# Attention and gated MLP on one core: row tiles 4 and 5 are loaded transposed, and the opening's loads and statistics stand in another order

## The chip, the core and the metric

The kernel runs on one core of a Trainium2 chip. A core has TensorE (PE in the profile; it multiplies matrices and, with an identity as operand, transposes), VectorE (DVE), ScalarE (ACT), GpSimd (POOL) and SyncE (SP), which here only issues transfers. Each engine works through its own list of instructions in order and waits on semaphores for the others. Transfers run on 16 DMA engines. The metric is the device time of one execution in microseconds (us); the time of a kernel is the median of its runs.

## The reference

x has 2048 rows (positions) of 512 numbers. Cut to what matters here:

```python
xn = _layernorm(x, axis=-1)              # every row: minus its mean, times its rstd
s = _A_ref(xn, A_wqkv, A_wo)             # qkv = xn @ wqkv; 32 heads, 8 positions back in steps of 2
g = _silu(_B_ref(xn, B_w_in, B_w_sp, B_b_sp, B_w_out))
return x + s * g
# _B_ref: z = gelu(xn @ w_in); z1 | z2 = its halves; z2 = layernorm(z2)
#         out = (z1 * (w_sp @ z2 + b_sp)) @ w_out
```

Everything begins with the normalised rows xn, and PE needs them with the 512 features on the partitions, that is, transposed.

## The kernel before

**Tiles.** Tile j of the 16 row tiles holds rows p * 16 + j, with p = 0 to 127 on the partitions. Matrices are multiplied in float32 accuracy by three products: every operand is split into a high part (an ACT copy to the type fp32r) and a low part (a DVE subtraction), and high x high, high x low and low x high are added. A tile against one group of 512 columns of wqkv takes 4 blocks of features x 3 = 12 matmuls of 512 columns. There are three such groups; the part of the program in question is the first 60 us, groups 0 and 1. Behind it come group 2, the two halves of the MLP and the spatial product (w_sp), with the attention's DVE and GpSimd work beside them, and the output projection.

**Two ways to a transposed tile.** Tiles 0 to 5 (`OPEN = 6`) come in by rows (`load_x`). DVE takes mean and variance (`stats_x`, L214 and L215), GpSimd the power -1/2 (`rstd_x`, L221), DVE subtracts the mean (and for tiles 4 and up multiplies by rstd) (`normal_x`, L228, L197), PE transposes four 128 x 128 blocks into a PSUM bank (`turned_x`, L234), ACT copies the high part (L235), DVE makes the low part (`low_x`, L240). For tiles 0 to 3 rstd is applied later.

Tiles 6 to 15 come in twice. By rows (`fetch_rows`, L257) only for their statistics (`row_stats`, L261 and L262). By columns from an input that holds x transposed (`fetch_cols`, L268), which needs the mean and rstd of each row along the free dimension, on every partition. They get there over DRAM: power on GpSimd (`rows_ready`, L272 and L273), a small DVE transpose of the table `mvx` of all tiles' statistics (`rows_out`, L244), four small stores of it to `mv_d` (L246), and one load that broadcasts it to all partitions (`rows_in`, L277). Then DVE subtracts and multiplies in two operations of 128 x 512 (`column_tile`, L286), ACT copies the high part (L289) and DVE makes the low part.

**What sets the order.** Instructions given through `pin` stay, on each engine, in the order in which the code is written: all the above, and the loads on SP. The products behind the opening (`product`, L395 to L397) and the evictions with their stores (`pair`, L443 and L452) are not pinned; the scheduler puts them where its own timeline has their operands ready. SP issues in order, so a load that waits for a free buffer holds up what stands behind it. Row tiles by `fetch_rows` have 6 buffers, column tiles 4, the broadcast rows 2, the small transpose's result 1.

**The opening** (`opening`, L301) writes PE's order out by hand: `times(j, ...)` (L314) gives single matmuls of tile j in group 0, and tile j + 1's transposes stand between tile j's high and low parts. `raw1` are the four loads of group 1's weights, which `weights(1, ...)` splits when the opening ends. The finished products of tiles 0 to 4 are kept in `first`; `pair(0, j)` evicts them two at a time.

## Time and profile before

| what | us |
|---|---|
| median of 3 runs | 692.48 |
| lowest, highest run | 691.8, 693.27 |
| the profiled execution, its own time | 692.16 |
| its span, first to last instruction | 690.3 |
| granted TensorE clock, mean | 1.000 |
| PE, DVE, ACT, POOL busy | 684.8, 619.8, 276.0, 216.8 |

The profile is of one execution, 692.16 us long, of which 690.3 lie between its first and last instruction. PE's busy time is a model of overlapping matmuls, so a busy PE says only that there was no hole in its work; how fast it advances is read from the distance between the starts of its instructions. In rows in order of time the columns are start, duration, engine, line, operation, tile written <- tiles read, shapes, count, and in brackets the idle time before and what ended it. SPq and ACTq are transfers issued by these engines; an issue's row says nothing of when the data lands. In rows of stretches the columns are the stretch, its length, the busy time of PE, PE's weight loads (PEld), DVE, ACT and POOL with counts, the granted clock, the share of the DMA engines and GB/s. A name in these rows leaves out tile numbers, so `qkv<-wqkv_0h` may be of any group, and 0 there is the block of features.

### The profile page before, as it was taken

The numbers are of one execution on the slowest core, as the hardware profiler recorded it, in microseconds if no ns is written. First come the engines' busy times: TensorE is split into PE (matmuls) and PEld (weight loads), VectorE is DVE, ScalarE is ACT, GpSimd is POOL, SyncE is SP. The second block draws the span as 40 slices with busy tenths as digits, with TensorE's granted clock in tenths as the row PEclk, the third lists the DMA queues.
The fourth block names the chain that finished last, engine by engine and source line by source line (L and its number), as shares of the span: only waits on it lengthen the run. The fifth ranks groups of instructions, "written<-read, shape, count | busy, mean of one in ns | idle before, by whom it ended". The sixth has DMA issues, their size and how long they took to land.

```text
span 690.3 us, 9237 instructions
## 1 busy us (share of the span) xinstructions
PE 684.8 (99%) x3080; PEld 572.5 (83%) x3080; DVE 619.8 (90%) x866; ACT 276.0 (40%) x458; POOL 216.8 (31%) x242
## 2 busy tenths in 40 slices
PE   9999999999999999999999999999999999999997
PEld 7888888888888899888888888888888888888886
DVE  6677869999989979798999999999999999999765
ACT  4343334224424256785434544432444444211432
POOL 3105837373443221223323222224021202552320
PEclk9999999999999999999999999999999999999999
DMA  8759899969999865267797859677576692663996
GB/s 281 257 180 299 292 359 388 334 218 370 404 414 355 324 207 180 97 207 249 232 397 285 328 195 319 202 237 262 171 270 238 219 325 89 205 186 126 308 309 252
DMA packets 102223, 182.43 MB, mean 264 GB/s; under 512 B 9184, under 2 KB 45152, under 8 KB 102176
## 3 DMA queue, kind: packets, MB, share of 16 engines
q1 hardware_dynamic: 56624, 102.21, 43.7%
q0 software_dynamic: 13824, 52.24, 20.9%
q10 hardware_dynamic: 31728, 27.40, 11.9%
q8 instruction: 24, 0.39, 0.2%
q14 instruction: 23, 0.19, 0.1%
HBM read 122.49 MB, written 59.32 MB: 263 GB/s over the span
## 4 chain that ended last, share of the span: by engine, by line
PE 99%; DMA 0%; DVE 0%; issue 0%
PE g L848 39%; PE qkv L395 6%; PE qkv L396 6%; PE qkv L397 6%; PE z L751 4%; PE z L750 4%; PE z L715 4%; PE z L714 4%; PE b L1089 4%; PE b L1091 4%; PE b L1090 4%; PE z L716 4%; PE z L749 3%; PE s L1089 2%; PE s L1091 2%; PE s L1090 2%
## 5 line engine op out<-in xcount | busy, mean ns | idle before, releaser
L643 POOL TENSOR_TENSOR pv<-pv 128x1024 f32<-128x1024 f32 x29 | 69.6, 2399 | 94.3 <-DVE pv L630 83.0
L583 DVE TENSOR_TENSOR pr<-k,q 128x2048 f32<-128x2048 f32 x32 | 74.7, 2333 | 1.5 <-DMA k<-qkv_d 1.4
L630 DVE TENSOR_TENSOR pv<-v,lg 128x2048 f32<-128x2048 f32 x32 | 74.5, 2329 | 0.6
L590 DVE TENSOR_REDUCE lg<-pr 128x128 f32<-128x2048 f32 x32 | 72.9, 2279 | 0.1
L657 POOL DMA_DIRECT2D o_d<-tt x32 | 17.9, 560 | 148.0 <-DVE tt L656 104.5
L443 ACT ACTIVATE stage<-qkv 128x512 f32<-128x512 f32 x40 | 23.0, 590 | 31.9 <-DMA qkv_d<-stage 20.2
L1100 ACT ACTIVATE bt<-b 128x512 f32<-128x512 f32 x16 | 9.5, 596 | 45.7 <-PE b L1091 45.7
L830 POOL DMA_DIRECT2D ol<-o_d x32 | 17.7, 554 | 28.9 <-DVE o_1l L204 6.0
L720 ACT ACTIVATE z1t<-z 128x512 f32<-128x512 f32 x28 | 15.5, 596 | 25.8 <-DMA z_d<-z1t 14.1
L761 DVE BATCH_NORM_STATS2 zst<-zt 128x6 f32<-128x448 f32 x32 | 19.3, 610 | 7.0 <-ACT zt L752 7.0
L751 PE MATMUL z<-w_0h,BIG 128*128 128x512 f32 x64 | 25.0, 391 | 0.0
L750 PE MATMUL z<-w_0l,BIG 128*128 128x512 f32 x64 | 25.0, 391 | 0.0
L286 DVE TENSOR_TENSOR xT<-xT,mr 128x512 f32<-128x512 f32 x20 | 14.9, 743 | 11.2 <-DMA mr<-mv_d 6.9
L775 ACT ACTIVATE zt<-zt,nmz,mvz 128x896 f32<-128x896 f32 x16 | 17.4, 1128 | 18.0 <-POOL nmz L769 18.0
L767 POOL TENSOR_TENSOR mvz<-mvz,nhalf 128x2 f32<-128x2 f32 x8 | 9.3, 1157 | 47.3 <-DVE mvz L764 47.3
L749 PE MATMUL z<-w_0h,BIG 128*128 128x512 f32 x60 | 23.3, 389 | 0.0
L648 DVE TENSOR_TENSOR pv<-pv 128x512 f32<-128x512 f32 x32 | 22.9, 714 | 0.0
L752 ACT ACTIVATE zt<-z 128x512 f32<-128x512 f32 (+1 forms) x32 | 16.0, 537 | 15.8 <-DMA sums_d<-sa 12.2
L751 PE MATMUL z<-w_1h,BIG 128*128 128x384 f32 x64 | 21.5, 336 | 0.0
L750 PE MATMUL z<-w_1l,BIG 128*128 128x384 f32 x64 | 21.5, 335 | 0.0
L403 POOL TENSOR_TENSOR sb<-sa,sb 128x512 f32<-128x512 f32 x12 | 19.8, 1647 | 5.4 <-DMA sb<-in_w_sp 5.0
L202 ACT ACTIVATE BIG<-zl 128x512 fp32r<-128x512 f32 x20 | 12.4, 630 | 20.7 <-DVE zl L921 20.6
(480 smaller groups left out, 2262.6 us busy)
## 6 DMA issues: line engine op xcount, KB each, us to landing
qkv_d<-stage ACTq DMA_DIRECT2D x24, 512.0 KB
v<-qkv_d POOLq DMA_DIRECT2D x14, 704.0 KB, 5.0
k<-qkv_d POOLq DMA_DIRECT2D x13, 704.0 KB, 6.3
sums_d<-sa POOLq DMA_DIRECT2D x14, 512.0 KB, 7.6
sums_d<-sb POOLq DMA_DIRECT2D x14, 512.0 KB, 9.4
z_d<-z1t ACTq DMA_DIRECT2D x14, 512.0 KB
zl<-z_d SPq DMA_DIRECT2D x12, 512.0 KB
tr<-t_d SPq DMA_DIRECT2D x12, 384.0 KB
```

The lines of the kernel that those rows point to most:

```text
L395: nc.tensor.matmul(pq, xh[:, k], wh, start=k == 0, stop=False)
L396: nc.tensor.matmul(pq, xh[:, k], wl, start=False, stop=False)
L397: nc.tensor.matmul(pq, xl[:, k], wh, start=False, stop=k == KB - 1)
L583: line(nc.vector.tensor_tensor(pr, taps(ks[u], j0), qb.unsqueeze(1).to_broadcast([P, W, NJ * CS]), op=ALU.mult))
L590: line(nc.vector.tensor_reduce(lgs[u][:, j0 * HS : (j0 + NJ) * HS].rearrange("p i w -> p w i"), pr.rearrange("p w (i d) -> p w i d", d=DH) ...
L630: line(nc.vector.tensor_tensor(pv.rearrange("p w (i d) -> p w i d", d=DH), taps(vs[u], j0).rearrange("p w (i d) -> p w i d", d=DH), lgs[u] ...
L643: eng.tensor_tensor(pv[:, 0:4], pv[:, 0:4], pv[:, 4:8], op=ALU.add)
L749: nc.tensor.matmul(pz, xh[:, k], wh, start=k == 0, stop=False)
L750: nc.tensor.matmul(pz, xh[:, k], wl, start=False, stop=False)
L751: nc.tensor.matmul(pz, xl[:, k], wh, start=False, stop=k == KB - 1)
L848: nc.tensor.matmul(pg, z[a], w[b], start=start and i == 0, stop=stop and i == 2, skip_group_check=seeded)
L1089: nc.tensor.matmul(pp[:, cols], hi, wh, start=k == 0, stop=False)
```

## The change

`OPEN` becomes 4. Tiles 4 and 5 join the tiles that come in by columns, so their eight PE transposes go; their statistics now make the trip over DRAM in a group of their own, (4, 6), and they get two loads more, one by rows and one by columns, four small stores and a broadcast load. Their products in group 0 and tile 5's first one leave the hand-written opening for `product`. Group 1's weights are loaded ahead of the rows of tiles 6 and up. Behind the opening, loads, statistics, broadcast rows and column tiles are written in another order, `pair(1, 0)` and `pair(1, 2)` stand ahead of `pair(0, 4)`, and the row loads and the column tiles are spread: column loads that wait for a buffer no longer stand ahead of the broadcast rows of tiles 9 to 12, and statistics of later tiles stand behind column tiles that are due.

```diff
--- before.py
+++ after.py
@@ -48,7 +48,7 @@
 WARM = 8
 RAW = 4
 WIDE = 8
-OPEN = 6
+OPEN = 4
 SYNC = mybir.DependencyInfo(mybir.DependencyClass.Sync, mybir.DependencyReason.DATA)
 NOSYNC = mybir.DependencyInfo(mybir.DependencyClass.NoSync, mybir.DependencyReason.DATA)
 TCKW = {"schedule_with_timeline_sim": True}
@@ -359,32 +359,36 @@
         times(1, (3, 0, 0), *[(k, 1, 0) for k in range(KB)], (2, 0, 1))
         times(0, (3, 0, 1))
         times(1, (3, 0, 1))
-        x += [load_x(j) for j in range(3, OPEN)]
-        for j in range(OPEN, OPEN + 4):
+        x.append(load_x(3))
+        for j in (4, 5):
             fetch_rows(j)
         raw1 = [fetch(wqkv[:, 1, k, :], GC, f"wqkv_1_{k}") for k in range(3)]
         raw1.append(t2("wqkv_1_3r", 1, tag="tz", bufs=1))
         pin(nc.sync.dma_start(raw1[3], wqkv[:, 1, 3, :]))
-        for j in range(3, OPEN):
-            xt = x[j]
-            stats_x(j, xt)
-            low_x(j - 1, p)
-            normal_x(j, xt)
-            if j - 1 < JC:
-                rstd_x(j - 1)
-            first.append(mm(f"qkv_0_{j - 1}"))
-            left.append(12)
-            times(j - 1, *[(k, 0, i) for i in range(2) for k in range(KB)])
-            p = turned_x(j, xt)
-            times(j - 1, *[(k, 1, 0) for k in range(KB)])
-            row_stats(OPEN + j - 3)
-        low_x(OPEN - 1, p)
-        for j in range(10, 13):
+        for j in (6, 7):
             fetch_rows(j)
-        for j in range(6, 10):
+        for j in (4, 5):
             fetch_cols(j)
-        rows_ready(6, 9)
-        rows_out((6, 9))
+        for j in (8, 9):
+            fetch_rows(j)
+        stats_x(3, x[3])
+        low_x(2, p)
+        normal_x(3, x[3])
+        rstd_x(2)
+        left.extend([12, 12])
+        first.append(mm("qkv_0_2"))
+        times(2, *[(k, 0, i) for i in range(2) for k in range(KB)])
+        p = turned_x(3, x[3])
+        times(2, *[(k, 1, 0) for k in range(KB)])
+        first.append(mm("qkv_0_3"))
+        times(3, *[(k, 0, i) for i in range(2) for k in range(KB)])
+        for j in (4, 5):
+            row_stats(j)
+        rows_ready(4, 6)
+        low_x(3, p)
+        times(3, *[(k, 1, 0) for k in range(KB)])
+        rstd_x(3)
+        rows_out((4, 6))
         return raw1
 
     def product(g, j, wg):
@@ -439,7 +443,7 @@
         stage = tmp.tile([P, 2 * GC], F32, tag="t35", name=f"stage_{g}_{j0}", bufs=3)
         sv = stage.rearrange("p (b j c) -> p b j c", b=NBLK, j=2)
         for j in (j0, j0 + 1):
-            pq = first[j] if g == 0 and j < OPEN - 1 else product(g, j, wgs[g])
+            pq = first[j] if g == 0 and j < OPEN else product(g, j, wgs[g])
             nc.scalar.activation(
                 sv[:, :, j % 2, :],
                 pq.rearrange("p (b c) -> p b c", b=NBLK),
@@ -455,36 +459,54 @@
     wgs = {0: [None] * KB}
     wgs[1] = weights(1, opening(wgs[0]))
     pair(0, 0)
+    for j in (10, 11):
+        fetch_rows(j)
+    rows_in(4, 6)
+    for j in (6, 7):
+        fetch_cols(j)
+    pair(0, 2)
+    for j in range(6, 9):
+        row_stats(j)
+    rows_ready(6, 9)
+    for j in (12, 13):
+        fetch_rows(j)
+    row_stats(9)
+    fetch_rows(14)
+    rows_out((6, 9))
+    column_tile(4)
+    column_tile(5)
+    fetch_rows(15)
     rows_in(6, 9)
-    for j in range(13, NT):
-        fetch_rows(j)
-    pair(0, 2)
-    for j in range(9, 13):
+    low_x(4, cols[4])
+    low_x(5, cols[5])
+    pair(1, 0)
+    for j in range(10, 13):
         row_stats(j)
     rows_ready(9, 13)
-    pair(0, 4)
+    for j in (8, 9):
+        fetch_cols(j)
     column_tile(6)
     rows_out((9, 13))
+    pair(1, 2)
     column_tile(7)
     low_x(6, cols[6])
-    for j in range(10, 12):
-        fetch_cols(j)
     rows_in(9, 13)
-    pair(1, 0)
+    fetch_cols(10)
+    low_x(7, cols[7])
+    fetch_cols(11)
+    pair(0, 4)
     for j in range(13, NT):
         row_stats(j)
     rows_ready(13, NT)
     column_tile(8)
-    low_x(7, cols[7])
-    fetch_cols(12)
     rows_out((13, NT), (0, JC))
-    pair(1, 2)
+    pair(1, 4)
     column_tile(9)
     low_x(8, cols[8])
     rows_in(13, NT)
+    fetch_cols(12)
     column_tile(10)
     low_x(9, cols[9])
-    pair(1, 4)
     for j in range(11, NT):
         if j + 2 < NT:
             fetch_cols(j + 2)
@@ -515,7 +537,7 @@
 
     pins[0] = False
     for g in range(1, NG):
-        for j in range(OPEN if g == 1 else 0, NT, 2):
+        for j in range(OPEN + 2 if g == 1 else 0, NT, 2):
             if g == 1 and j == NT // 2:
                 pins[0] = True
                 wgs[2] = weights(2)
```

Where it moves instructions, in three places. In the rows below, names carry their numbers: `qkv_1_0` is group 1, tile 0; `wqkv_1_0h` is group 1, feature block 0, high part; `xt_4` the transposed tile 4; the last number is only a buffer's.

PE, from tile 3's last high matmul in the opening on, before:

```order
L316 MATMUL qkv_0_3_267<-wqkv_0_3l_168,BIG_98 128x512
L234 MATMUL xt_4_276<-ident_85,x_4_209 128x128 x4
L316 MATMUL qkv_0_3_267<-wqkv_0_0h_130,BIG_98 128x512
L316 MATMUL qkv_0_3_267<-wqkv_0_1h_144,BIG_98 128x512
L316 MATMUL qkv_0_3_267<-wqkv_0_2h_150,BIG_98 128x512
L316 MATMUL qkv_0_3_267<-wqkv_0_3h_167,BIG_98 128x512
L316 MATMUL qkv_0_4_296<-wqkv_0_0h_130,BIG_98 128x512
```

and now:

```order
L316 MATMUL qkv_0_3_259<-wqkv_0_3l_168,BIG_98 128x512
L399 MATMUL qkv_1_0_362<-wqkv_1_0h_289,BIG_98 128x512
L399 MATMUL qkv_1_1_376<-wqkv_1_0h_289,BIG_98 128x512
L399 MATMUL qkv_1_2_416<-wqkv_1_0h_289,BIG_98 128x512
L399 MATMUL qkv_1_3_430<-wqkv_1_0h_289,BIG_98 128x512
L316 MATMUL qkv_0_3_259<-wqkv_0_0h_130,BIG_98 128x512
L316 MATMUL qkv_0_3_259<-wqkv_0_1h_144,BIG_98 128x512
L316 MATMUL qkv_0_3_259<-wqkv_0_2h_150,BIG_98 128x512
L316 MATMUL qkv_0_3_259<-wqkv_0_3h_167,BIG_98 128x512
L400 MATMUL qkv_1_0_362<-wqkv_1_0l_290,BIG_98 128x512
```

Where tile 4's transposes stood, group 1 begins on tiles 0 to 3; all its 48 matmuls on these tiles come before tile 4's first.

SP, behind the opening's first loads, before:

```order
L526 DMA qkv_d_75<-zpad_111 16x8x64 x2
L209 DMA x_4_209<-in_x 128x512
L209 DMA x_5_211<-in_x 128x512
L257 DMA x_6_213<-in_x 128x512
L257 DMA x_7_215<-in_x 128x512
L257 DMA x_8_217<-in_x 128x512
L257 DMA x_9_219<-in_x 128x512
L176 DMA wqkv_1_0r_221<-in_wqkv 128x512
L176 DMA wqkv_1_1r_223<-in_wqkv 128x512
```

and now, from the row loads of tiles 6 and 7 (the four loads of group 1's weights stand ahead of them):

```order
L257 DMA x_6_221<-in_x 128x512
L257 DMA x_7_223<-in_x 128x512
L268 DMA xT_4_225<-in_x_t 128x512
L268 DMA xT_5_227<-in_x_t 128x512
L257 DMA x_8_229<-in_x 128x512
L257 DMA x_9_231<-in_x 128x512
L246 DMA mv_d_83<-mvt_4_283 4x32 x4
L257 DMA x_10_309<-in_x 128x512
L257 DMA x_11_311<-in_x 128x512
L277 DMA mr_4_313<-mv_d_83 128x512
L268 DMA xT_6_315<-in_x_t 128x512
L268 DMA xT_7_317<-in_x_t 128x512
```

Group 1's first weight stands right behind tile 5's rows instead of behind tile 9's, and the first stores of statistics come behind 20 loads of 256 KB instead of 25.

DVE, behind tile 2's low part and tile 3's subtraction, before:

```order
L261 BN_STATS st_6_255<-x_6_213 128x6
L262 BN_AGGR mvx_94<-st_6_255 128x2
L214 BN_STATS st_4_258<-x_4_209 128x6
L215 BN_AGGR mvx_94<-st_4_258 128x2
L220 TENSOR_SCALAR mvx_94<-mvx_94 128x1
L240 TENSOR_TENSOR BIG_98<-xt_3_245,BIG_98 128x4x128
L197 TENSOR_SCALAR x_4_209<-x_4_209,mvx_94 128x512
```

and now:

```order
L261 BN_STATS st_4_268<-x_4_209 128x6
L262 BN_AGGR mvx_94<-st_4_268 128x2
L261 BN_STATS st_5_271<-x_5_211 128x6
L262 BN_AGGR mvx_94<-st_5_271 128x2
L272 TENSOR_SCALAR mvx_94<-mvx_94 128x2
L240 TENSOR_TENSOR BIG_98<-xt_3_249,BIG_98 128x4x128
L220 TENSOR_SCALAR mvx_94<-mvx_94 128x1
L244 STREAM_TRANSPOSE mvt_4_283<-mvx_94 128x32
L204 TENSOR_TENSOR wqkv_1_0l_290<-wqkv_1_0r_213,wqkv_1_0h_289 128x512
```

Tile 5's statistics take tile 4's place, and the first small transpose of the statistics comes behind tile 3's low part instead of behind tile 5's.

## The prediction

> **What bounds the kernel now.** I read the page's first and fourth parts, then who TensorE (PE) waited for, then its instructions in order of time around the change.
>
> ```profile
> span 690.3 us, 9237 instructions
> PE 684.8 (99%) x3080; PEld 572.5 (83%) x3080; DVE 619.8 (90%) x866; ACT 276.0 (40%) x458; POOL 216.8 (31%) x242
> PE 99%; DMA 0%; DVE 0%; issue 0%
> ...
> PE warm L296 <- POOL ident masks.py:199: 1.3, 1, 1.3
> PE xt L234 <- DVE x L228: 0.3, 1, 0.3
> ```
>
> The first three are lines of the page (the third is the chain that ended last), the last two are all of PE's waits. PE works without a hole from 5.4 us to its end; its two waits lie in the first 5.4 us, in instructions that the change leaves alone. So nothing can be won by removing a wait. Only taking instructions off PE, or letting them follow each other faster, shortens the run, and any new wait of PE is paid in full.
>
> PE in order of time (start, duration):
>
> ```profile
> 13.75 0.40 PE L316 MATMUL qkv<-wqkv_0h,BIG 128*128 128x512 f32 x1
> ...
> 18.81 0.60 PE L234 MATMUL xt<-ident,x 128*128 128x128 f32 x4
> 19.17 0.48 PE L316 MATMUL qkv<-wqkv_0h,BIG 128*128 128x512 f32 x1
> 19.48 0.40 PE L316 MATMUL qkv<-wqkv_1h,BIG 128*128 128x512 f32 x1
> ...
> 22.07 0.60 PE L234 MATMUL xt<-ident,x 128*128 128x128 f32 x4
> 22.43 0.49 PE L316 MATMUL qkv<-wqkv_0h,BIG 128*128 128x512 f32 x1
> 22.75 0.39 PE L316 MATMUL qkv<-wqkv_1h,BIG 128*128 128x512 f32 x1
> ...
> 23.92 1.38 PE L395 MATMUL qkv<-wqkv_0h,BIG 128*128 128x512 f32 x5
> 25.14 0.40 PE L397 MATMUL qkv<-wqkv_0h,BIG 128*128 128x512 f32 x1
> ...
> 42.60 0.39 PE L395 MATMUL qkv<-wqkv_0h,BIG 128*128 128x512 f32 x1
> ```
>
> The unit is the spacing of starts, not the duration, because matmuls overlap. From 25.14 to 42.60 stand 77 matmuls: 17.46 / 77 = 0.227 us each.
>
> **The change part by part.** *Removed from PE: two groups of four transposes, tiles 4 and 5.* The first group and the matmul behind it take 19.48 - 18.81 = 0.67 us; less one matmul's 0.227 that is 0.44. The second: 22.75 - 22.07 = 0.68, so 0.45. Together 0.90. If only the distance to the next matmul's start goes (0.36 each), it is 0.72.
>
> [...]
>
> *Pace of the opening.* Tile 4's and 5's products leave the hand-written opening for the ordinary product. From 19.48 to 22.07 there are 11 matmuls in 2.59 us, 0.235 each, 0.10 more than at 0.227. Tile 3's share of these stays, so I take half, 0.05. At 23.92 five matmuls take 25.14 - 23.92 = 1.22 instead of 1.13: they wait on a weight that ScalarE (ACT) splits only then. With the earlier split this 0.09 goes. Bounds of both terms: 0 to 0.19.
>
> Sum for PE: -0.90 - 0.05 - 0.09 = -1.04, say **-1.0 us**, between -0.72 and -1.09, provided that PE meets no new wait. The matmuls of tiles 4 and 5 are the same number as before.
>
> *When PE now asks for what.* Until 18.81 PE's order is unchanged. Then stand four matmuls on the first weight of group 1, four of tile 3, and the rest of group 1 on tiles 0 to 3: 52 in all, so tile 4's high part is asked for at 18.81 + 52 x 0.227 = 30.6, its low part four matmuls later, at 31.5. Tile 6 follows 48 matmuls behind tile 4, at 41.5 (before: 42.60).
>
> *Group 1's weights, earlier.* They must be split by 18.8 (high) and 20.6 (low).
>
> ```profile
> 13.79 0.68 DVE L261 BATCH_NORM_STATS2 st<-x 128x6 f32<-128x512 f32 x1
> 14.61 0.66 DVE L214 BATCH_NORM_STATS2 st<-x 128x6 f32<-128x512 f32 x1
> 16.21 0.60 ACT L235 ACTIVATE BIG<-xt 128x512 fp32r<-128x512 f32 x1 [1.23 <-PE xt L234]
> 16.84 0.69 DVE L240 TENSOR_TENSOR BIG<-xt,BIG 128x512 fp32r<-128x512 f32 x1 [1.17 <-ACT BIG L235]
> 18.13 0.55 POOL L221 TENSOR_TENSOR mvx<-mvx,nhalf 128x1 f32<-128x1 f32 x1 [1.83 <-DVE mvx L220]
> 23.20 0.62 ACT L202 ACTIVATE wqkv_0h<-wqkv_0r 128x512 fp32r<-128x512 f32 x1
> 25.21 0.65 DVE L204 TENSOR_TENSOR wqkv_0l<-wqkv_0r,wqkv_0h 128x512 fp32r<-128x512 f32 x1
> ```
>
> The first weight's load takes the SP place that tile 6's rows held, and those had landed when VectorE (DVE) read them at 13.79 without a wait. ACT is free at 16.81; plus 0.62 the first high part is there at 17.4, 1.4 us early. DVE's low part stands behind the small transpose of the statistics: 18.6 + 0.65 = 19.2, also 1.4 early. This costs nothing; the cover is ACT's and DVE's idle time (1.23 and 1.17 in these rows).
>
> *Tiles 4 and 5 by columns.* Their normalisation now hangs on a round trip through DRAM: statistics, power on GpSimd, small transpose, four stores, one broadcast load, two DVE operations, ACT, DVE. Before, tiles 6 to 8 were the first to make it:
>
> ```profile
> 23.95 0.16 DVE L272 TENSOR_SCALAR mvx<-mvx 128x3 f32<-128x3 f32 x1
> 24.18 0.86 POOL L273 TENSOR_TENSOR mvx<-mvx,nhalf 128x3 f32<-128x3 f32 x1 [3.70 <-DVE mvx L272]
> 25.08 0.21 DVE L244 STREAM_TRANSPOSE mvt<-mvx 128x32 f32<-128x32 f32 x1 [0.98 <-POOL mvx L273]
> 25.32 1.34 SPq L246 DMA_DIRECT2D mv_d<-mvt  x4
> 28.57 0.35 SPq L277 DMA_DIRECT2D mr<-mv_d  x1
> 33.47 1.42 DVE L286 TENSOR_TENSOR xT<-xT,mr 128x512 f32<-128x512 f32 x2 [2.39 <-DMA mr<-mv_d]
> 34.92 0.64 ACT L289 ACTIVATE BIG<-xT 128x512 fp32r<-128x512 f32 x1 [1.41 <-DVE xT L286]
> 36.23 0.68 DVE L240 TENSOR_TENSOR BIG<-xT,BIG 128x512 fp32r<-128x512 f32 x1
> ```
>
> Now the statistics of 4 and 5 stand where 13.79 and 14.61 are, but the small transpose reads the whole table and so waits for tile 3's power too, behind the subtraction at 16.84: that power ends, as before's at 18.13 + 0.55, at about 18.4 to 18.7. Transpose at 18.5. From there by the rows: 33.47 - 25.08 = 8.4 us to the broadcast rows in use, so 26.9. DVE is free by then: four weight subtractions (0.6 apart), four statistics (0.8 apart) and a small transpose from 18.7 end at about 25. Then 36.23 - 33.47 = 2.8 to the start of the low part, with tile 5's two operations ahead of it as tile 7's were here, and 0.68 for it: 30.3, against 31.5. The high part: 34.92 + 0.64 - 33.47 = 2.1, so 29.0 against 30.6; ACT has the evictions of two products ahead of it, which PE ends by 27.1. So the rows give PE no wait, with **1.2 us to spare**.
>
> What may use it up is the transfer queue: in the row of before the stores met an empty one.
>
> ```profile
> 20.00:22.00 2.00, 2.00 (x10) 1.56 (x9) 1.88 (x4) 0.74 (x2) 0.48 (x1) 1.00 1.09 391
> 22.00:24.00 2.00, 2.00 (x13) 1.43 (x11) 0.71 (x3) 1.29 (x3) 0.00 (x0) 1.00 1.08 361
> 24.00:26.00 2.00, 2.00 (x10) 1.66 (x10) 1.02 (x5) 1.87 (x4) 0.86 (x1) 1.00 0.48 146
> ```
>
> The last two columns are DMA share and GB/s: 25 loads of 256 KB kept the queue full to 24 us. Now 20 loads stand ahead of the stores; five fewer are 1.3 MB, 3.5 us at 375 GB/s, so the queue empties near 20.5 to 21 and the stores issued from 18.7 may lie behind up to 2 us of loads. Bounds: wait of 0 (an undisturbed round trip) to 2.0 - 1.2 = 0.8 us. I take 0, being nearer to the row than to a queue that is full throughout.
>
> [...]
>
> *Late next: tiles 6 to 8.* Their stores come behind the first broadcast load on SP. From its use at 26.9 the same 8.4 and 3.5 give 38.8, against 41.5. Tile 9, before:
>
> ```profile
> 41.99 0.33 SPq L277 DMA_DIRECT2D mr<-mv_d  x1
> 46.08 1.42 DVE L286 TENSOR_TENSOR xT<-xT,mr 128x512 f32<-128x512 f32 x2 [4.51 <-DMA mr<-mv_d]
> 49.34 0.69 DVE L240 TENSOR_TENSOR BIG<-xT,BIG 128x512 fp32r<-128x512 f32 x1
> ```
>
> Its low part ended at 50.0, about a microsecond ahead of PE. This broadcast load stood on SP behind column loads that waited for a buffer; now it is issued ahead of them, which more than makes up for PE's coming 1 us sooner. The four DVE multiplications more, two small transfers and two column loads lie beside PE.
>
> **The rivals.** (1) *The round trip eats part of the gain*: stores behind loads as by the upper bound, a wait of 0.3 to 1.0 at tile 4; 691.5 to 692.4. For it: the full queue. Against: 1.2 us of room.
>
> (2) *Slower: the broadcast rows of tiles 4 and 5 come too late.* One mechanism, at PE's first low matmul of tile 4. It costs PE what the landing exceeds 31.5 - 0.68 - 2.8 = 28.0. At 29.0 the gain is gone, from 30.4 the kernel is over 0.2% slower; at 31 the time is 692.5 - 1.0 + 3.0 = 694.5. This needs the round trip to take 12 us instead of 8.4. For it: both legs pass through DRAM while loads run, and six loads and a 512 KB store follow close. Against: the load at 41.99 brought twice these bytes in 4.1.
>
> (3) *A transpose is worth its record, 0.27 us, eight times*: 690.3. Against: the spacing above.
>
> (4) *It does not do what it says for the time*: the transposes go but PE's matmuls fill the place at a slower pace, 0.235 for the 24 of tiles 4 and 5: 0.2 back, 691.7; not to be told from the forecast.
>
> **How the numbers follow.** The profiled execution took 692.16 us, span 690.3 and 1.86 around it; the sum makes it 691.1. The runs' median is 692.48, 0.32 above. I set the forecast between 691.1 and 692.48 - 1.0 = 691.5, at **691.4 us**. 0.2% of the time is 1.38 us, about what a measurement here can tell from no change, and the gain is 1.0: the likeliest outcome is a gain too small to call.
>
> Chances: the forecast (with 4) 0.66; rival 1 0.14; rival 2, with any wait of its kind elsewhere, 0.12; rival 3 0.08. The three runs of before lie 1.5 us apart, so 0.20 of the forecast's 0.66 may read as faster, with 0.06 of rival 3: faster 0.26. Slower is rival 2: 0.12. Within 0.2% is the rest: 0.46 + 0.14 + 0.02 = 0.62. Range 690.4 to 692.7, which leaves out most of rival 2 and the far end of 3; the forecast's own is 691.0 to 691.8.
>
> **What would show it.** Right: eight PE records fewer, no wait of PE behind 5.4 us, tile 6's first matmul near 41.5, group 1's first split near 16.8, broadcast rows in use by 28. Wrong: a wait of PE on DVE or ACT at tile 4 near 31; broadcast rows past 28; the first group 1 weight arriving past 18.8; or the gain given back past 60 us, where DVE's order for the attention shifts.

## The result, and the profile after

The change made the kernel **slower: a median of 700.78 us (699.63 to 702.61) against 692.48 (691.80 to 693.27), a ratio of 1.0123 [1.0104, 1.0141]**. The forecast was 691.4 us, with a range of 690.4 to 692.7. The profiled execution of the changed kernel took 701.48 us, with a span of 699.6, so it is 9.3 us longer than that of before from its first to its last instruction.

The page of the changed kernel and PE's waits in it:

```profile
span 699.6 us, 9243 instructions
PE 686.9 (98%) x3072; PEld 572.2 (82%) x3072; DVE 615.3 (88%) x868; ACT 275.8 (39%) x458; POOL 217.3 (31%) x241
PE 59%; DVE 17%; DMA 16%; issue 4%; ACT 1%; POOL 1%; SPq 1%; ACTq 0%; DVEq 0%; POOLq 0%
...
PE z L771 <- ACT z1t L742: 2.8, 1, 2.8
PE qkv L401 <- DVE BIG L240: 2.3, 2, 1.2
PE z L736 <- ACT z1t L742: 1.6, 2, 1.2
```

The eight transposes are gone (3072 records where 3080 stood). The chain that ended last was 99% PE before and is 59% PE now: it passes through DVE and transfers, because PE has waits that it did not have. All of them behind 10 us in order of time, after the first row, which is tile 6's first matmul (42.60 before):

```profile
41.38 0.39 PE L399 MATMUL qkv<-wqkv_0h,BIG 128*128 128x512 f32 x1
...
48.52 0.50 PE L401 MATMUL qkv<-wqkv_0h,BIG 128*128 128x512 f32 x1 [1.09 <-DVE BIG L240]
58.65 0.50 PE L401 MATMUL qkv<-wqkv_0h,BIG 128*128 128x512 f32 x1 [1.21 <-DVE BIG L240]
...
202.63 0.50 PE L736 MATMUL z<-BIG,w_5h 128*128 128x512 f32 x1 [0.43 <-ACT z1t L742]
209.59 0.50 PE L736 MATMUL z<-BIG,w_lasth 128*128 128x512 f32 x1 [1.22 <-ACT z1t L742]
223.56 0.50 PE L771 MATMUL z<-w_0h,BIG 128*128 128x512 f32 x1 [2.78 <-ACT z1t L742]
```

The start of a stage's first matmul, in both profiled executions, shows where the 9.3 us came from:

| first matmul of | before | after | later by |
|---|---|---|---|
| tile 6 (group 0) | 42.60 | 41.38 | -1.22 |
| MLP, first half (z1) | 140.52 | 142.20 | +1.68 |
| MLP, second half (z2) | 216.68 | 223.56 | +6.88 |
| spatial product (g) | 294.21 | 302.84 | +8.63 |
| MLP's output (b) | 566.26 | 575.15 | +8.89 |
| output projection (s) | 642.42 | 651.31 | +8.89 |

So the gain that was forecast arrived, 1.22 us by 41 us, and was lost twice. **Loss 1** lies between 41 and 62 us: two waits, 2.30 us, and 0.6 more, nearly all of it right around them (the two steps between starts into and out of a wait take 1.81 us, 47.05 to 48.86, and 1.94, 57.05 to 58.99, instead of 2 x 0.227). **Loss 2** lies in the z1 stage, some 80 us behind the opening that the change rewrites: the stage took 76.16 us and takes 81.36, and the next one is 1.75 longer. The rows show that second part: behind the wait of 2.78 the matmuls stand 0.43 apart instead of 0.227, and two stretches there give the granted clock (the third number from the end):

```profile
225.04 0.63 PE L773 MATMUL z<-w_0h,BIG 128*128 128x512 f32 x1
225.47 0.63 PE L771 MATMUL z<-w_0h,BIG 128*128 128x512 f32 x1
...
223.00:230.00 7.00, 6.44 (x21) 5.19 (x22) 6.97 (x8) 3.13 (x6) 3.96 (x4) 0.76 0.98 349
225.00:226.00 1.00, 1.00 (x4) 0.77 (x3) 0.97 (x2) 0.53 (x2) 1.00 (x2) 0.50 0.91 227
```

0.76 over 7 us at either 0.50 or 1.00 is 7 x 0.24 / 0.50 = 3.4 us at half the clock, which loses 1.7 us.

### The profile page after: what moved, and what is told of

It is laid out like the page before. It is cut to its first block, busy times and chain, and to the rows that moved or that the text cites. A ratio compares the mean times of both kernels' runs of the same rounds, so it can differ in the third digit from the quotient of the medians.

```text
span 699.6 us, 9243 instructions
## 1 busy us (share of the span) xinstructions
PE 686.9 (98%) x3072; PEld 572.2 (82%) x3072; DVE 615.3 (88%) x868; ACT 275.8 (39%) x458; POOL 217.3 (31%) x241
## 3 DMA queue, kind: packets, MB, share of 16 engines
q0 software_dynamic: 13824, 52.24, 20.9%
## 4 chain that ended last, share of the span: by engine, by line
PE 59%; DVE 17%; DMA 16%; issue 4%; ACT 1%; POOL 1%; SPq 1%; ACTq 0%; DVEq 0%; POOLq 0%
PE g L870 39%; DVE pr L605 4%; PE z L772 4%; PE z L773 4%; PE z L771 4%; DMA qkv_d<-stage 3%; DMA sg<-b_d 3%; DVE lg L612 3%; DMA ol<-o_d 2%; DMA sb<-in_w_sp 2%; DVE pv L652 2%; PE b L1113 2%; PE b L1111 2%; PE b L1112 2%; PE qkv L316 2%
## 5 line engine op out<-in xcount | busy, mean ns | idle before, releaser
L605 DVE TENSOR_TENSOR pr<-k,q 128x2048 f32<-128x2048 f32 x32 | 77.6, 2426 | 12.3 <-DMA k<-qkv_d 8.7
L742 ACT ACTIVATE z1t<-z 128x512 f32<-128x512 f32 x28 | 15.5, 597 | 41.6 <-DMA z_d<-z1t 32.8
L771 PE MATMUL z<-w_0h,BIG 128*128 128x512 f32 x60 | 24.0, 400 | 2.8 <-ACT z1t L742 2.8
L286 DVE TENSOR_TENSOR xT<-xT,mr 128x512 f32<-128x512 f32 x24 | 16.4, 688 | 11.0 <-DMA mr<-mv_d 6.4
L773 PE MATMUL z<-w_0h,BIG 128*128 128x512 f32 x64 | 25.7, 402 | 0.0
L407 POOL TENSOR_TENSOR sb<-sa,sb 128x512 f32<-128x512 f32 x12 | 17.1, 1424 | 14.5 <-DMA sb<-in_w_sp 14.3
L202 ACT ACTIVATE BIG<-zt 128x512 fp32r<-128x512 f32 (+2 forms) x24 | 16.1, 694 | 13.5 <-DVE zt L812 13.4
```

The source lines that it names most:

```text
L202: first_ = pin(nc.scalar.activation(hi, src, AF.Copy))
L605: line(nc.vector.tensor_tensor(pr, taps(ks[u], j0), qb.unsqueeze(1).to_broadcast([P, W, NJ * CS]), op=ALU.mult))
L771: nc.tensor.matmul(pz, xh[:, k], wh, start=k == 0, stop=False)
L773: nc.tensor.matmul(pz, xl[:, k], wh, start=False, stop=k == KB - 1)
```

## The experiments

From `for j in range(11, NT)` on, the two programs have the same instructions, one for one. They differ there only in the order in which the scheduler put the unpinned ones on each engine. So the opening of one kernel can be run with the later order of the other. In the kernels below with a *held order*, every engine's instructions from that point on (in the kernels below that move single instructions or edit the opening, from the end of `opening` on) are chained in the order of a table, taken from the one kernel or the other, by dependences that set the order of issue:

```diff
+    for one, two in zip(row, row[1:]):
+        tc.add_manual_dep(two, one.name, NOSYNC, reason="order by table")
```

Holding an order costs nothing by itself: *old_sums_at_13* below, which is before with its own order held and one hook moved, is at 0.9994 of before. A kernel's ratio is against before, run beside it on the same chip.

### Is it the opening, or the order behind it?

*new_opening_old_order*: the changed opening, and before's order held behind it.

> After's program up to row tile 10; from row tile 11 to the end every engine's instructions are held in the order that they have in before. Theory A (late chain: row tiles 8 to 12 are normalised late, so the spatial sums on GpSimd start 4.7 us late, and everything that hangs on them at 200 to 225 us): both losses stay, 699 to 701 us. Rival B (the loss of 7 us at 200 to 225 us is the order that the scheduler found for the attention and the z1 stage after the change, whatever the opening): only the loss in the first 60 us stays, 693 to 695 us.

Measured: 697.55 us, 1.0069 [1.0054, 1.0084], between the two ranges. The z1 stage takes 76.16 us again, but it begins at 146.54, later than in the changed kernel (142.20).

*old_opening_new_order*: before's opening, and the changed kernel's order held behind it.

> Before's program up to row tile 10; from row tile 11 to the end every engine's instructions are held in the order that they have in after. Theory A: before's time, 692 to 693 us, because the tiles and the sums are on time. Rival B: the loss at 200 to 225 us appears without the new opening, 698 to 700 us.

Measured: 698.82 us, 1.0104 [1.0076, 1.0131]. PE's only long wait in it, by the table of waits, is the one that was longest in the changed kernel (this file is longer, so L813 is the changed kernel's L771, and L784 its L742):

```profile
PE z L813 <- ACT z1t L784: 2.8, 1, 2.8
```

Each half alone slows the kernel, and the two add up to more than the whole change (1.0123), as the loss in the opening differs between kernels (see below). The order does it with an opening of which no instruction was changed.

*new_sums_at_11* and *old_sums_at_13*: the first theory for loss 2 was that GpSimd's sums of w_sp, which are hooked to a row tile, begin too late. The hook is moved, with the order held:

```diff
-        if j == 12:
+        if j == 11:
```

(13 in the second, which is made from before.)

> After with every engine's order held as it is; only the GpSimd sums wait for row tile 11 on VectorE instead of row tile 12, so that they start near 52.4 us instead of 58.7. Theory A: the loss at 200 to 225 us goes, the one in the first 60 us stays: 693 to 695 us. Rival B: 700 to 701 us, no change.

> Before with every engine's order held as it is; only the GpSimd sums wait for row tile 13 on VectorE instead of row tile 12, so that they start near 59.9 us instead of 54.0. Theory A: the loss at 200 to 225 us appears in before, 697 to 700 us. Rival B: 692 to 693 us, no change.

Measured: 705.01 us, 1.0186 [1.017, 1.0202], for the earlier hook in the changed kernel, and 691.89, 0.9994 [0.9985, 1.0004], for the later one in before. Both fall outside what the theory allows. In the changed kernel the sums then began at 52.81 us instead of 58.66 (53.95 before), and the z1 stage still took 80.83 us; the further loss lies in the opening, where z1 begins at 146.04. In before they began at 60.96 without a loss. The theory fell.

### Which stage's order?

*old_new_order_qkv* and *old_new_order_z1*: before, with the changed kernel's order held only up to the end of the QKV products, and only from the z1 stage on. *new_old_order_z1*: the changed kernel, with before's order held from the z1 stage on.

> Before's program up to row tile 10. Behind it TensorE, and ScalarE and GpSimd up to the end of the query, key and value products, stand in after's order; everything from the z1 stage on in before's. Theory C (the loss at 200 to 225 us is made in the z1 stage, where the scheduler put the sums' additions and the splits of the weights differently on VectorE, ScalarE, GpSimd and SyncE): before's time, 692 to 693 us. Rival D (it is made earlier: by the order of evictions and copies on ScalarE VectorE gets its first key and query tiles late, and never catches up): 696 to 699 us.

> The other half: before's program, with after's order only from the z1 stage on (all of VectorE's and SyncE's differences, those of ScalarE and GpSimd that lie there). Theory C: 697 to 699 us, as much as with the whole order (698.8). Rival D: 692 to 693 us.

> After with its own order up to the end of the query, key and value products, and before's order from the z1 stage on. Theory C: the loss at 200 to 225 us goes, that of the first 60 us stays (1.7): 693 to 695 us. Rival D: 699 to 701 us.

Measured: 692.08 us, 1.0002 [0.9986, 1.0018]; 699.22, 1.0096 [1.0068, 1.0124]; 694.96, 1.0037 [1.0016, 1.0058]. The order of the QKV stage costs nothing, with before's opening. The order from z1 on has loss 2 whole, and given back, it leaves loss 1 alone: z1 to z2 takes 76.16 us again in *new_old_order_z1*, as before, though its z1 stage begins 2.95 us later (143.47).

### Which instructions?

Loss 2 can be followed in the rows in order of time. DVE before: the splits of the first two blocks of the second half's weights, w2_0_0 and w2_1_0 (the rows leave the numbers out), and attention's score product.

```profile
153.02 0.68 DVE L204 TENSOR_TENSOR w_0l<-w_0r,w_0h 128x512 fp32r<-128x512 f32 x1
153.83 0.65 DVE L204 TENSOR_TENSOR w_0l<-w_0r,w_0h 128x512 fp32r<-128x512 f32 x1
155.19 2.28 DVE L583 TENSOR_TENSOR pr<-k,q 128x2048 f32<-128x2048 f32 x1
```

DVE in the changed kernel: the same three, the product now between the splits, and the sums' first addition.

```profile
157.84 0.67 DVE L204 TENSOR_TENSOR w_0l<-w_0r,w_0h 128x512 fp32r<-128x512 f32 x1
158.77 2.27 DVE L605 TENSOR_TENSOR pr<-k,q 128x2048 f32<-128x2048 f32 x1
161.57 0.67 DVE L204 TENSOR_TENSOR w_0l<-w_0r,w_0h 128x512 fp32r<-128x512 f32 x1
...
172.46 0.69 DVE L407 TENSOR_TENSOR sb<-sa,sb 128x512 f32<-128x512 f32 x1 [4.87 <-DMA z_d<-z1t]
```

SP's issues, changed kernel, and below them before:

```profile
158.53 4.07 SPq L176 DMA_DIRECT2D w_1r<-in_w_in  x2
163.07 0.41 SPq L412 DMA_DIRECT2D sa<-in_w_sp  x1
```

```profile
153.72 1.11 SPq L176 DMA_DIRECT2D w_1r<-in_w_in  x2
155.94 0.38 SPq L408 DMA_DIRECT2D sa<-in_w_sp  x1
```

The two weight loads took 1.11 us to issue and take 4.07: they wait for a raw buffer (a ring of four) that the split at 161.57 frees. That is 2.96 more, as much as the two splits have moved apart (0.81 before, 3.73 now). The sums' loads stand behind them on SP and are issued 20.9 us after z1's first matmul instead of 15.4. DVE then stands 4.87 us for the first addition, with attention's next product behind it. The row names a store as what ended this wait; in *old_split_moved*, below, the rows of the first two additions name the sums' loads. ACT, which evicts z1 through the buffers that the sums use (`t4`), is the next to be late, and PE waits for ACT:

```profile
208.94 1.09 ACT L742 ACTIVATE z1t<-z 128x512 f32<-128x512 f32 x2 [5.88 <-DMA sums_d<-sb]
221.62 1.28 ACT L742 ACT_TABLE_LOAD   x1 [3.92 <-DMA sums_d<-sa]
```

In the changed order two things moved on DVE here: the split of w2_1_0 back, from ahead of a score product (`pr_0`) to behind it with a step of attention's `pv`, and the first addition forward, ahead of the next one (`pr_4`). Whether each alone makes the loss was tried in both directions. DVE's order, *new_two_moved_back* against the changed kernel (the minus rows are where the changed order had them):

```diff
 TENSOR_TENSOR w_0_0l<-w_0_0r,w_0_0h 128x512
+TENSOR_TENSOR w_1_0l<-w_1_0r,w_1_0h 128x512
 TENSOR_TENSOR lg<-lg,mx 128x256
 TENSOR_TENSOR pr_0<-k_1,q_1 128x2048
 TENSOR_TENSOR pv_0<-pv_0 128x512
-TENSOR_TENSOR w_1_0l<-w_1_0r,w_1_0h 128x512
...
 TENSOR_REDUCE lg<-pr_0 128x8x16
+TENSOR_TENSOR pr_4<-k_1,q_1 128x2048
+TENSOR_TENSOR pv_4<-pv_4 128x512
+TENSOR_TENSOR w_2_0l<-w_2_0r,w_2_0h 128x512
 TENSOR_TENSOR sb_0<-sa_0,sb_0 128x512
-TENSOR_TENSOR pr_4<-k_1,q_1 128x2048
-TENSOR_TENSOR pv_4<-pv_4 128x512
-TENSOR_TENSOR w_2_0l<-w_2_0r,w_2_0h 128x512
```

*new_split_moved_back* has the upper half of this alone, *new_add_moved_back* the lower half alone; *old_two_moved* and *old_split_moved* put both, and the split alone, into before in the other direction.

> After, every engine's order held, with two instructions of VectorE put back where before has them: the split of the weight block w2_1_0 ahead of the score product instead of behind it, and the first addition of the spatial sums (sb_0) behind the score product, the fold and the next split instead of ahead of them. Theory E (the whole loss at 200 to 225 us comes from these two: the late split frees a raw buffer late, SyncE's weight load waits for it and holds the sums' loads back until 163 us, and the addition put ahead makes VectorE wait 4.9 us for them): VectorE's wait at 172 us goes, 694 to 696 us. Rival F (the loss is spread over the scheduler's other 120 moved instructions): 699 to 701 us.

> Before, every engine's order held, with the same two instructions of VectorE moved to where after has them. Theory E: VectorE waits about 5 us for the sums' loads near 165 us and the loss appears, 697 to 699 us. Rival F: 692 to 693.5 us.

> After, every engine's order held, with only the split of the weight block w2_1_0 put back ahead of the score product. If the late split is the cause (SyncE's weight load waits for its raw buffer and holds the sums' loads): the sums' loads are issued near 159 us instead of 163, VectorE's wait for them shrinks from 4.9 to under 1.5 us, 696 to 698 us. If the addition put ahead is: 699.5 to 701 us.

> After, every engine's order held, with only the first addition of the sums put back behind the score product, the fold and the next split. If the addition put ahead is the cause: VectorE has 3.7 us of other work while the sums' loads come, its wait shrinks to about 1.2 us, 696 to 698 us. If the late split is: the loads still come at 172 us, 699 to 701 us.

> Before, every engine's order held, with one instruction of VectorE moved: the split of the weight block w2_1_0 behind the score product, 4.6 us later, where after has it. If the late split alone makes the second loss: SyncE's second weight load of that pair takes about 4 us instead of 1, the sums' loads are issued near 160 us instead of 156, TensorE waits on ScalarE's z1 evictions between 195 and 220 us, 695.5 to 698.5 us. If it needs the addition put ahead as well: VectorE has other work until 167 us and waits 2 to 3 us, 692 to 694 us.

| kernel | us | ratio to before | z1 stage, us |
|---|---|---|---|
| new_two_moved_back | 697.59 | 1.0080 [1.0062, 1.0097] | 76.16 |
| old_two_moved | 697.57 | 1.0079 [1.0052, 1.0106] | 81.32 |
| new_split_moved_back | 699.66 | 1.0100 [1.0072, 1.0128] | 76.16 |
| new_add_moved_back | 703.57 | 1.0159 [1.0141, 1.0178] | 83.84 |
| old_split_moved | 699.66 | 1.0094 [1.0067, 1.0121] | 81.49 |

By their times alone the three made from the changed kernel decide nothing: 697.59 lies between the two ranges, 699.66 in the range that was set for the addition as the cause, and 703.57 above both. Their z1 stages do.

The split decides it. Moved by itself into before it makes the whole loss, 1.0094, about 1 us above its range, with the same chain in SP's issues and DVE's rows:

```profile
153.87 4.88 SPq L242 DMA_DIRECT2D w_1r<-in_w_in  x2
...
176.60 0.69 DVE L469 TENSOR_TENSOR sb<-sa,sb 128x512 f32<-128x512 f32 x1 [5.93 <-DMA sb<-in_w_sp]
...
PE z L781 <- ACT z1t L787: 2.1, 1, 2.1
```

Put back in the changed kernel it ends it: 0.93 us for the two weight loads, 0.18 us idle ahead of the addition, no wait of PE on z1t (*new_split_moved_back*):

```profile
159.94 0.93 SPq L242 DMA_DIRECT2D w_1r<-in_w_in  x2
...
169.30 0.72 DVE L473 TENSOR_TENSOR sb<-sa,sb 128x512 f32<-128x512 f32 x1 [0.18 <-issue]
```

The addition moved back alone is worse than the changed kernel, 703.57: the loads are as late as there, and the addition now waits 6.98 us at 182.48.

The whole times of the two kernels with the split put back hold less of this than their z1 stages do, since their opening lost more in the profiled executions: z1 begins at 145.95 and 143.84 instead of 142.20. With this opening unmended, z1 begins 1.7 to 6.0 us later than before in the six kernels that have it unedited (the changed one among them). The two largest (5.4 in *new_split_moved_back*, 6.0 in *new_opening_old_order*) have a wait of PE of 2.71 and 2.10 us near 61 us where the others have 1.0 to 1.2, and behind it the granted clock falls, to 0.50 from 63 to 65 us in both. *new_split_moved_back*, the wait and a stretch behind it:

```profile
60.80 0.50 PE L467 MATMUL qkv<-wqkv_0h,BIG 128*128 128x512 f32 x1 [2.71 <-DVE BIG L306]
...
63.00:65.00 2.00, 2.00 (x6) 1.62 (x5) 1.97 (x4) 0.96 (x2) 0.18 (x1) 0.50 0.60 157
```

Why that wait is longer in these two was not settled.

### The opening

PE takes tiles 6 to 10 in order, twelve matmuls each, and the third matmul of a tile is the first to need its low part. The wait at 48.52 is 26 matmuls behind tile 6's first and so at tile 8's low part. The wait at 58.65 is 38 further on; two high matmuls of another tile stand between, and it ends with tile 11's low part (57.91 + 0.68). DVE's rows in the changed kernel, the multiplications of tile 9 with tile 8's low part behind them, and those of tile 12 with tile 11's:

```profile
46.45 1.42 DVE L286 TENSOR_TENSOR xT<-xT,mr 128x512 f32<-128x512 f32 x2 [0.26 <-DMA mr<-mv_d]
47.79 0.68 DVE L240 TENSOR_TENSOR BIG<-xT,BIG 128x512 fp32r<-128x512 f32 x1
...
56.58 1.42 DVE L286 TENSOR_TENSOR xT<-xT,mr 128x512 f32<-128x512 f32 x2 [4.25 <-DMA xT<-in_x_t]
57.91 0.68 DVE L240 TENSOR_TENSOR BIG<-xT,BIG 128x512 fp32r<-128x512 f32 x1
```

Before, tile 8's low part, and the later multiplications that waited for their columns, tile 13's:

```profile
47.41 0.69 DVE L240 TENSOR_TENSOR BIG<-xT,BIG 128x512 fp32r<-128x512 f32 x1
...
57.79 1.42 DVE L286 TENSOR_TENSOR xT<-xT,mr 128x512 f32<-128x512 f32 x2 [3.91 <-DMA xT<-in_x_t]
```

Tile 8's low part was ready at 48.10 before, and PE asked for it at 42.60 + 26 x 0.227 = 48.5: 0.4 us to spare. Now PE asks 1.2 us sooner, and the low part is ready 0.4 later, since tile 9's broadcast rows came at 46.45 instead of 46.08. That is the first wait. The second comes from tile 12's column load, which the change moves behind the broadcast rows of tiles 13 to 15: before, the wait for columns fell on tile 13, one tile further on. It takes both, the late columns and tile 11's low part standing behind them.

A third place was near its limit. Broadcast rows of tiles 6 to 8: SP's issues, the wait that the table of SP's waits (20 to 36 us) gives there, and, below, DVE's first use of them, all in the changed kernel:

```profile
25.09 6.92 SPq L246 DMA_DIRECT2D mv_d<-mvt  x4
32.97 0.34 SPq L277 DMA_DIRECT2D mr<-mv_d  x1
...
SPq L246 <- DMA qkv_d<-stage: 5.6, 1, 5.6
```

```profile
37.80 1.42 DVE L286 TENSOR_TENSOR xT<-xT,mr 128x512 f32<-128x512 f32 x2 [4.47 <-DMA mr<-mv_d]
```

The four small stores of these tiles' statistics took 6.92 us to issue instead of 1.34. For 5.6 of it SP stood for a transfer that has nothing to do with them, the second 512 KB store of QKV results, which ACT issued at 21.50. In the program each of these transfers waits for the one eight places ahead of it (they use eight semaphores in turn), and the changed order puts one of the stores eight places behind that result store. The trace shows it: the result store's landing was complete at 31.03 us, and the second of the four stores, which uses the same semaphore, was issued at 31.05. The rows are in use 12.7 us behind the first store's issue instead of 8.2 (33.47 against 25.32 before). In this profile PE still had no wait at tile 6. In four other kernels with this opening it waited 0.3 to 0.6 us near 42.7, the third matmul of tile 6.

*new_rows_behind_stores*: the row loads of tiles 12 to 14 are moved behind these stores, the rest of the changed kernel's order held.

```diff
-    for j in (12, 13):
-        fetch_rows(j)
...
-    fetch_rows(14)
...
     rows_out((6, 9))
+    for j in (12, 13, 14):
+        fetch_rows(j)
```

> After with every engine's order held, but on SyncE the row loads of tiles 12 to 14 stand behind the four stores of tiles 6 to 8 instead of ahead of them. If loss 1 comes from the stores of tiles 6 to 8 issued late: the broadcast load of tiles 6 to 8 is issued before 29 us instead of 32.97, both waits of TensorE near 48.5 and 58.7 us (1.1 and 1.2) go, 697 to 698.5 us. If the lateness of tiles 8 and 12 has another cause (the eight stores ahead of tile 12's column load): the second wait stays, 699 to 700 us. If the loss at 200 to 225 us hangs on this lateness as well: 692 to 694 us.

Measured: 702.83 us, 1.0139 [1.0111, 1.0167], above all three ranges. The stores were issued in 1.30 us, but a row load ahead of the broadcast load now stands eight places behind the result store, and waited 3.0 us for it. The rows were in use at 37.89, as late as before the edit:

```profile
24.43 1.30 SPq L312 DMA_DIRECT2D mv_d<-mvt  x4
30.96 0.36 SPq L343 DMA_DIRECT2D mr<-mv_d  x1
...
SPq L323 <- DMA qkv_d<-stage: 3.0, 1, 3.0
```

The next four are made from *new_old_order_z1* (before's order from z1 on), so that only the opening is left. *new_low_first* finishes a column tile's low part before the next tile's multiplications, and *new_low_first_col12* also fetches tile 12's columns earlier:

```diff
+    low_x(8, cols[8])
+    fetch_cols(12)
     rows_out((13, NT), (0, JC))
     pair(1, 4)
-    low_x(8, cols[8])
...
-    fetch_cols(12)
+    low_x(9, cols[9])
     column_tile(10)
-    low_x(9, cols[9])
```

(`low_x(j - 1)` likewise ahead of `column_tile(j)` in the loop; *new_low_first* has it without the two rows on tile 12.) *new_load_seven_behind* takes tile 7's column load and the row loads of tiles 12 to 15 out of the way, so that the broadcast load comes seven places behind the result store, and *new_seven_low_first* joins all of these:

```diff
-    for j in (6, 7):
-        fetch_cols(j)
+    fetch_cols(6)
...
     rows_in(6, 9)
+    for j in (12, 13, 14, 15):
+        fetch_rows(j)
+    fetch_cols(7)
```

> After with before's order from the z1 stage on (694.96 us), and in row tiles 8 to 15 the subtraction that makes a tile's low part stands ahead of the next tile's normalisation on VectorE, instead of behind it. If the three waits of TensorE for low parts below 60 us (2.8 in all) come from that order: they go, 691 to 692.5 us. If the column tiles themselves come too late: VectorE waits for tile 12's column load as before and TensorE for tile 12 instead, 694 to 695.5 us.

> The same, and on SyncE the column load of tile 12 stands ahead of the eight stores of the last statistics, as in before. If TensorE's waits hang on both: 691 to 692 us, the change's own gain of about 1 us; tile 12 is normalised near 52 us instead of 57. If the load moved ahead makes the stores and so tile 13 late: a wait of TensorE near 63 us, 693 to 695 us.

> After with before's order from the z1 stage on (694.96 us); on SyncE, behind the column load of tile 6, come the four stores of tiles 6 to 8 and their broadcast load, and only then the row loads of tiles 12 to 15 and the column load of tile 7. So the broadcast load is the seventh transfer behind the store of the first result stage, not one that waits for it. If that wait is what makes tiles 6 to 12 late: the load is issued near 28 us instead of 33 and used near 33 instead of 38 to 39, TensorE's waits at 42.9, 50.2 and 60 us go, 691 to 692.5 us. If the two legs through DRAM are slow by themselves (as when the stores were issued early and the load took 6.9 us): used at 36 us or later, 694 to 695.5 us.

> The same, and each tile's low part ahead of the next tile's normalisation on VectorE from tile 8 on, and the column load of tile 12 ahead of the eight stores of the last statistics. If all of the first loss lies in these three places: no wait of TensorE behind 10 us, 691 to 691.8 us, 0.1 to 0.2% faster than before. If something else is left (the evictions, the weights of group 1): 692.5 to 694 us.

| kernel | us | ratio to before | z1 begins (140.52 before) |
|---|---|---|---|
| new_old_order_z1 | 694.96 | 1.0037 [1.0016, 1.0058] | 143.47 |
| new_low_first | 694.25 | 1.0040 [1.0021, 1.0059] | 142.04 |
| new_low_first_col12 | 693.55 | 1.0027 [1.0012, 1.0042] | 141.78 |
| new_load_seven_behind | 692.62 | 1.0005 [0.9993, 1.0017] | 141.91 |
| new_seven_low_first | **691.54** | **0.9980 [0.9965, 0.9995]** | 139.15 |

With the broadcast load free of the result store, it is issued at 28.48 instead of 32.97. All of PE's waits that are left in *new_seven_low_first*:

```profile
28.48 0.34 SPq L343 DMA_DIRECT2D mr<-mv_d  x1
...
PE warm L362 <- POOL ident masks.py:199: 1.3, 1, 1.3
PE qkv L382 <- ACT BIG L301: 0.2, 1, 0.2
```

Both end in the first 7 us, ahead of the part that was changed. z1 begins 1.37 us earlier than before, and the kernel is faster than before by 0.20% [0.05, 0.35]: what the removed transposes were forecast to be worth. It is the fastest of all versions. Either mend alone left some of the loss. By its time *new_low_first* can't be told from *new_old_order_z1*, and both it and *new_low_first_col12* fell in the range that was set for another cause: the two long waits are gone, but one of 0.38 us at 42.75, on tile 6's low part, is left, and behind 47.64 and 59.69 four matmuls each take 1.5 to 1.6 us instead of 0.91, at tiles whose parts come just late. *new_load_seven_behind* has a wait of 2.33 at 49.75, on tile 8's low part, which still stands behind tile 9's multiplications.

### What stays open

*new_mended*: the changed kernel's own order from z1 on, with the split put back and both mends of the opening.

> After's own order on every engine to the end, with the mends alone: the broadcast load of tiles 6 to 8 seven places behind the result store, the low parts ahead of the next tile, the column load of tile 12 ahead of the eight stores, and the split of w2_1_0 put back. If the two causes are all there is: 691 to 692 us, no wait of TensorE behind 10 us. If other parts of the scheduler's new order cost something that the late split hid: 693 to 695 us.

Measured: 696.10 us, 1.0044 [1.0028, 1.0061], above both ranges. Its z1 and z2 begin at 139.06 and 215.52, earlier than before (140.52 and 216.68), but the spatial product waits for ACT, and the granted clock falls to 0.51 behind that:

```profile
295.62 0.50 PE L935 MATMUL g<-wsp_0h,BIG 128*128 128x512 f32 x1 [0.89 <-ACT g L953]
297.80 0.50 PE L935 MATMUL g<-wsp_0h,BIG 128*128 128x512 f32 x1 [1.22 <-ACT g L953]
...
298.50:302.00 3.50, 3.50 (x10) 2.69 (x9) 2.69 (x6) 2.67 (x4) 1.36 (x3) 0.51 0.84 201
```

From the spatial product's first matmul to the MLP's output it takes 276.33 us instead of 272.04. So the changed order has a third loss behind the other two. The changed kernel itself does not show it; *new_rows_behind_stores*, with the same order there, has waits of 0.30 and 1.22 us at the same place. Which of the moved instructions makes it was not tried.

## Why the prediction was wrong, by its steps

The section on the change names three places where instructions move, all in the first 60 us. The scheduler had moved others behind them, and there lies most of the loss.

**PE bounds the kernel, and any new wait is paid in full: right,** and more than in full. The wait of 2.78 us cost another 1.7 in slower matmuls behind it.

**The sum for PE, -1.0 us: right.** Tile 6's first matmul was forecast at 41.5 and came at 41.38, 1.22 us ahead of before, a little past the upper bound of 1.09; the profiles of the seven kernels with before's opening begin z1 between 140.08 and 140.83, so the excess means nothing. *new_seven_low_first*, where no new wait hides it, begins z1 1.37 earlier.

**Group 1's weights, forecast 1.4 us early at 17.4: right;** the first high part was there at 17.21 (16.59 + 0.62), and PE did not wait for it.

**Tiles 4 and 5 by columns, no wait: right.** The broadcast rows were in use at 26.18 (forecast 26.9), 7.8 us behind the stores at 18.38 (8.15 before, 25.32 to 33.47); PE did not wait at tile 4. With that **rival 1** and **rival 2 at its place** did not happen. But the ground on which the step stood was wrong too. It expected the queue to empty only near 20.5 to 21; in the changed kernel it was nearly idle as the stores came:

```profile
18.00:20.00 2.00, 2.00 (x10) 1.66 (x9) 1.86 (x4) 1.35 (x3) 0.10 (x1) 1.00 0.26 77
```

With the queue at 0.26 of its share and 77 GB/s, what a backlog of loads would have cost the stores was not shown.

**Late next, tiles 6 to 9: this step failed.** It looked at tile 9, found about a microsecond to spare, and held the earlier broadcast load to be worth "more than" PE's coming sooner. The load was issued 0.4 us earlier (41.59) and used 0.4 later. The tile that decided was 8, whose low part stands on DVE behind tile 9's multiplications and had 0.4 us to spare. PE's gain of 1.2 us was more than that, and 1.09 of it went at once. Every tile's margin had to be set against the gain, not the one that looked nearest. Tile 12's column load, which the change moves back on SP, was not in the sum at all; it took 1.21 us at tile 11's low part. The 8.4 for tiles 6 to 8 was wrong too. It gave rows in use at 26.9 + 8.4 = 35.3 and tile 6's low part at 38.8; they came at 37.80 and about 41.2 (40.56 + 0.69), 0.6 us before PE's third matmul of tile 6 at 41.83. The trip took 12.7 us from the stores' issue at 25.09, as the step asked how long it takes and not what the stores' issue waits for.

**What lies behind 60 us was costed at nothing: this is the larger failure.** The prediction took the program behind the opening as it was, since the diff does not touch it, and named "DVE's order for the attention" only as what might prove it wrong. The scheduler placed the unpinned instructions anew, and one of them, the split of one weight block, was put behind a score product, 2.9 us further from its neighbour. Of the 9.3 us in the profile, 6.95 belong to it (5.20 in the z1 stage, 1.75 behind). That the order differs there could be read in the two programs before the run; what it costs could not, but the place was not in the sum, with no bound on it either. The chance of 0.12 for any wait of this kind looks low for a change that lets the scheduler move the rest of the program.

**Rivals 3 and 4** concerned the price of the transposes. -1.22 at tile 6, the pace of the opening with it, is 0.15 us for each of the eight, nearer the spacing's 0.11 than the record's 0.27 (a median of 0.273 us for the 24 transposes in the profile of before).

## What to carry to other kernels

After an edit, compare the order of the whole program, not of the part that was edited: where a scheduler places the rest, an instruction a hundred microseconds behind the edit can free a buffer later, hold up a queue of loads and cost several times the gain, as the split at 161.57 us did here (6.95 us against 1.22). For every transfer that is moved, look at what its issue waits for, its turn of semaphores included (5.6 us here), before the time of its trip. When a change comes out slower although its own term arrived, hold the order of one version under the other and move single instructions: here that showed one subtraction to cost 6.5 us (1.0094), and left the change with its 0.2% gain.

## What the runs showed of the chip

**Behind some of PE's holes the granted clock was halved, behind others not.** Behind PE's wait of 2.78 us it was 0.50 for about 3.4 us, and matmuls stood 0.43 us apart instead of 0.227. A drop to 0.50 or 0.51 followed the waits of 2.71 and 2.10 us near 61 us (above), one of 2.14 in *old_split_moved*, and the two of 0.89 and 1.22 in *new_mended*; the stretches around each of these four drops (61 to 67 us twice, 208 to 214, 298 to 302) lose 1.70 to 1.72 us, again 3.4 us at half the clock. None followed a wait of 2.33 in *new_load_seven_behind* or one of 2.92 in *new_rows_behind_stores*, where it stood at 1.00. A stretch behind the wait in *old_split_moved*, *new_load_seven_behind* and *new_rows_behind_stores*:

```profile
210.00:212.00 2.00, 2.00 (x6) 1.52 (x6) 2.00 (x2) 1.28 (x1) 0.54 (x2) 0.50 1.03 397
```

```profile
50.00:52.00 2.00, 2.00 (x10) 1.62 (x10) 1.97 (x4) 1.19 (x3) 0.00 (x0) 1.00 0.13 20
```

```profile
224.00:226.00 2.00, 1.96 (x8) 1.61 (x9) 2.00 (x2) 1.88 (x4) 1.82 (x1) 1.00 0.99 361
```

So the length of the hole alone does not decide: 2.10 was followed by a drop, 2.33 and 2.92 were not. What else decides was not shown. The drop that was worked out above cost about 1.7 us.

**The order of issue coupled transfers of two engines that share no data.** Four stores of statistics, 1.3 us of issuing, took 6.92 because a 512 KB store that another engine had issued stood eight places ahead of one of them: SP waited 5.6 us for it. A row load eight places behind it waited 3.0 (*new_rows_behind_stores*). With the broadcast load seven places behind, it was issued at 29.47 us in *new_load_seven_behind* and at 28.48 in *new_seven_low_first* instead of 32.97.
